# Weight rows in runs of four, x turned by every fourth column, and keys loaded as pairs of groups: one edit to a fused attention and expert kernel

## The chip, the cores and the metric

The kernel runs on one core of a Trainium2 chip. The metric is the device time of one execution in microseconds (us); lower is better. The kernel before takes 197.68 us in the median of three runs (197.22 to 197.88).

## The reference, cut to what matters

Attention over pooled keys and values, then a router that sends each row to one of eight experts, then that expert's two matrix products:

```python
# q, k, v: [8, 8, 576, 64] (batch, head, position, dim)
k_p = k.reshape(B, H, 72, 8, D).mean(axis=3)      # 72 groups of 8 positions
v_p = v.reshape(B, H, 72, 8, D).mean(axis=3)
attn = softmax(q @ k_p^T / sqrt(D))               # [576, 72] for each head
x = (attn @ v_p).transpose(0, 2, 1, 3).reshape(4608, 512)
...
logits = normalized(x) @ normalized(expert_emb).T / tau
e = argmax(logits); gate = softmax(logits)[e]
out[row] = gate * (relu(x[row] @ w1[e]) @ w2[e])  # w1 [8, 512, 1024], w2 [8, 1024, 512]
```

All inputs and the output are float32. The kernel works in float16 on the chip; the loads issued by POOL change the type on the way.

## The kernel before, in words

The work is done batch by batch (b = 0 to 7, 576 rows each). For a batch: V and K come as tiles of 72 partitions (one partition for each group of 8 positions), Q as 128 partitions. DVE adds up the 8 positions of a group (steps VA, VB for V, KA, KB for K; `halve` at L496, `k_fold` at L503). TensorE turns the pooled keys (step KT, `kt`, L606) and DVE copies them out of PSUM into the tile kpT (step KE, L622). Q is turned by DVE (QT, L595). Scores (SC, L636), exponentials on ACT (EX, L644), the product with V (PV, L682) and the normalization (XM, L410 and L411) give x, a tile of 128 rows by 512 columns in float16.

Five such chunks of x make a batch. `transpose_rows` (XT, L419) turns a chunk in four pieces of 128 columns: the piece is TensorE's stationary operand and an identity is streamed past it; `transpose_last` (L425) does the same for the last 64 rows. The copies XE put the turned pieces in xt, [128, 4, 576]. The router (RT, L434) multiplies pieces of xt with the turned expert table enT. An early guess of the batch's expert comes from the mean of the pooled values (GM, GL: `guess` at L565, also with enT), so that the weights can be asked for in good time.

The expert's layers: `h_mm` (H, L766) accumulates four products with a slice of w1 as the stationary operand and xt streamed; `h_relu` (HE) makes hT; `y_mm` and `yl_mm` (Y, YL; L778, L785) multiply hT with w2; YE scales the rows, and SP stores them (ST, SL). Weights sit in four slots for w1 and four for w2, keys, values and queries in two each.

The order of instructions on each engine is written out by hand in a table (TABLES: names of steps for PE, DVE, ACT, POOL and SP). A planner walks the table with estimated costs to choose buffers and, in the first 62 us, the number of filler products (`keep_warm`, L903, products of a tile of ones whose result nobody reads) ahead of a PE step that would wait. These numbers are fixed when the program is built. All loads are issued by POOL, in the order of its table; POOL's loads take eight completion semaphores in turn (DMASW0 to DMASW7), and a load waits until the load eight places before it has landed.

Of the kernel before, what the change touches and what calls it, by code (L numbers as in the profile page):

```python
# [260 lines left out]
def kernel(  # L261
# [27 lines left out]
    NW = 4  # L289
    ND = 2  # L290
# [13 lines left out]
    w2_r = [ring(f"w2{i}", 1, [128, 4, 2, DM], FP16) for i in range(NW)]  # L304
# [37 lines left out]
    enT = const.tile([128, 4, E], FP16)  # L342
# [73 lines left out]
    def transpose_rows(x, pt):  # L416
        xf = x.rearrange("p a r d -> p (a r d)")
        for w in range(4):
            nc.tensor.transpose(out=pt.bitcast(FP16)[:, ts(w, 128)], in_=xf[:, ts(w, 128)],  # L419
                                identity=ident_h)  # L420

    def transpose_last(x, pt):
        xf = x.rearrange("p a r d -> p (a r d)")
        for w in range(4):
            nc.tensor.matmul(out=pt[:, ts(w, 64)], lhsT=xf[:, ts(w, 128)],  # L425
                             rhs=ident_h[:, 64:128], start=True, stop=True)
# [28 lines left out]
    def attention(b, base, xt):  # L455
# [8 lines left out]
        for c, src, raw in (("V", v, vr), ("K", k, kr)):  # L464
            if b == 0:
                add(n(c, 0), 'POOL', 0.9, 0.0,
                    lambda src=src, raw=raw: load_rows(src, b, raw.tile, 0, 64),
                    takes=[raw], mode=(16, 2.78 if c == "V" else 2.7, 1.2), late=0.9)
                add(n(c, 1), 'POOL', 0.6, 0.0,
                    lambda src=src, raw=raw: load_rows(src, b, raw.tile, 64),  # L470
                    uses=[raw], mode=(8, 1.25 if c == "V" else 0.6, 1.2),
                    late=0.9 if c == "V" else 2.4)
            else:
                add(n(c), 'POOL', 0.8, 0.0,
                    lambda c=c, src=src, raw=raw: note(n(c), load_rows(src, b, raw.tile)),
                    takes=[raw], mode=wire(ROWS_DMA), late=1.1)
# [15 lines left out]
        def by_group(t):  # L492
            return t.rearrange("g (a h) (c e) -> g a h c e", a=NQ, c=2)
# [5 lines left out]
        def k_fold():  # L499
            t = kr.tile  # L500
            halve(t, 2)
            for a in range(NQ):
                nc.vector.tensor_tensor(  # L503
                    out=kp_rows()[:, a], in0=by_group(t[:, :, 0])[:, a],
                    in1=by_group(t[:, :, 1])[:, a], op=ALU.add)
# [96 lines left out]

        def kt(heads=range(NQ)):
            for a in heads:
                for c in range(2):
                    nc.tensor.transpose(  # L606
                        out=pk.tile.bitcast(FP16)[:, ts(2 * a + c, G)],
                        in_=kp.tile[:, a, c].rearrange("g h e -> g (h e)"),
                        identity=ident_h[0:G, 0:G])
# [10 lines left out]
        else:  # L620
            add(n("KT"), 'PE', 0.14, pr(0.0), kt, [n("KB"), "PRE"], takes=[pk], uses=[kp], late=0.22)
            add(n("KE"), 'DVE', 0.2, pr(-0.1), lambda: nc.vector.tensor_copy(  # L622
                out=kpT.tile[:, :, :, 0:G],
                in_=pk.tile.bitcast(FP16)[:, 0:2 * NQ * G].rearrange(
                    "p (a c g) -> p a c g", a=NQ, c=2)), [n("KT")], takes=[kpT], uses=[pk],
# [137 lines left out]
    def h_mm(xt, w1, w, c0, c1, p):  # L763
        w1v = w1.rearrange("p k (w c r) -> p k w r c", r=2, c=128)
        for kk in range(4):
            nc.tensor.matmul(out=p[:, 0:c1 - c0], lhsT=w1v[:, kk, w // 2, w % 2, :],  # L766
# [9 lines left out]
    def y_mm(hT, w2, c, p):  # L776
        for w in range(8):
            landing[f"Y{c}"] = nc.tensor.matmul(  # L778
                out=p, lhsT=hT[w][:, ts(c, 128)], rhs=w2[:, w // 2, w % 2, :],
                start=(w == 0), stop=(w == 7))  # L780

    def yl_mm(hT, w2, p, at=1):
        for w in range(8):
            for r in range(2):
                nc.tensor.matmul(out=p[ts(r, 64), ts(r * at, DH)],  # L785
                                 lhsT=hT[w][:, 512:S], rhs=w2[:, w // 2, w % 2, ts(r, DH)],
# [14 lines left out]
    def half_chunk(n, b, c, r, w2, hT, hs, g, o_b):  # L801
# [104 lines left out]
    def prelude():  # L906
# [30 lines left out]
        nc.vector.tensor_copy(out=enT, in_=p.bitcast(FP16)[:, 0:4 * E].rearrange(  # L937
            "p (w e) -> p w e", e=E))
# [237 lines left out]
```

## Time and the profile before

| | |
|---|---|
| median of three runs | 197.68 us (197.22 to 197.88) |
| the profiled execution's own time, and its span | 197.28 us, 195.7 us |
| mean granted TensorE clock | 0.997 |
| PE busy | 188.8 us (96%) |
| DVE, ACT, POOL busy | 148.1 us (76%), 126.8 us (65%), 42.4 us (22%) |
| loads issued by POOL (queue q0) | 21904 packets, 28.85 MB, 85.3% of 16 engines' time |

The span runs from the first to the last instruction; 1.6 us of the execution's time lie outside it. A matmul's recorded duration holds its whole way through the array, and matmuls follow each other sooner than that: how fast PE really works is read from the distance between the starts of rows in a timeline.

### The profile page before, as it was taken

What the parts mean: (1) busy time and instruction counts of PE and PEld (TensorE: products, weight loads), DVE (VectorE), ACT (ScalarE), POOL (GpSimd) and SP (SyncE); (2) the same over time, 40 slices, a digit from 0 to 9 for tenths busy, and PEclk for the clock granted to TensorE, in tenths of its full rate; (3) what the DMA queues carried; (4) which work ended last, traced back from release to release, by engine and by line L of the source; (5) the groups of instructions that cost most, each with busy time, mean ns of one, the idle gap of its engine ahead of it and who ended that gap; (6) DMA issues with size and microseconds to landing.
All of it is one profiled execution on the core that took longest, in us unless ns stands there. A gap on an engine that the chain in (4) does not pass through costs nothing.

```text
span 195.7 us, 5369 instructions
## 1 busy us (share of the span) xinstructions
PE 188.8 (96%) x2099; PEld 125.8 (64%) x2100; DVE 148.1 (76%) x428; ACT 126.8 (65%) x295; POOL 42.4 (22%) x59
## 2 busy tenths in 40 slices
PE   7999999999999999999999999999999999999990
PEld 4784787556865566656685567467765668567740
DVE  1266899499989799898989899599789437846750
ACT  4007637789787887769884868588866776156330
POOL 7445000530650023440410142011200302002000
PEclk9999999999999999999999999999999999999998
DMA  3999999999999999999999999999969699227762
GB/s 40 186 195 192 207 210 207 176 210 208 210 207 211 208 210 187 199 207 208 211 212 272 253 201 158 221 238 232 173 135 316 170 221 212 77 57 274 286 215 94
DMA packets 27982, 38.69 MB, mean 198 GB/s; under 512 B 4264, under 2 KB 14760, under 8 KB 27952
## 3 DMA queue, kind: packets, MB, share of 16 engines
q0 software_dynamic: 21904, 28.85, 85.3%
q1 hardware_dynamic: 5824, 9.26, 13.8%
q8 instruction: 17, 0.28, 0.5%
q10 hardware_dynamic: 224, 0.20, 0.4%
q14 instruction: 13, 0.11, 0.1%
HBM read 61.88 MB, written 9.44 MB: 364 GB/s over the span
## 4 chain that ended last, share of the span: by engine, by line
PE 87%; DVE 8%; issue 1%; ACT 1%; DVEq 0%
PE pb L766 26%; PE pb L778 22%; PE pa L766 7%; PE pb L903 7%; PE pa L636 6%; PE pa L682 5%; PE pb L785 3%; PE pb L419 3%; DVE qT L595 2%; PE pb L434 1%; PE pa L419 1%; DVE x L411 1%; DVE vr L496 1%; PE pa L778 1%; DVE kr L496 1%
## 5 line engine op out<-in xcount | busy, mean ns | idle before, releaser
L766 PEld LDWEIGHTS <-w 128*128 128x128 f16 x512 | 47.5, 98 | 14.6 <-issue 3.3
L778 PE MATMUL pb<-w,hT 128*128 128x512 f16 x240 | 56.6, 379 | 0.0
L766 PE MATMUL pb<-xt,w 128*128 128x288 f16 (+2 forms) x392 | 56.6, 286 | 0.0
L644 ACT ACTIVATE at<-pa 72x576 f16<-72x576 f32 (+2 forms) x64 | 38.6, 642 | 11.4 <-PE pa L636 11.2
L778 PEld LDWEIGHTS <-hT 128*128 128x128 f16 x248 | 22.6, 97 | 24.4 <-issue 1.7
L705 ACT ACTIVATE sq<-x 128x512 f16<-128x512 f16 x40 | 25.2, 629 | 10.2 <-DVE x L411 7.9
L791 ACT ACTIVATE y<-pb,gm_all 128x512 f32<-128x512 f32 (+2 forms) x34 | 21.2, 628 | 12.0 <-PE pb L778 4.8
L411 DVE TENSOR_TENSOR x<-pa,r_all 128x512 f16<-128x512 f32 x38 | 26.3, 691 | 2.2
L772 ACT ACTIVATE hT<-pb 128x288 f16<-128x288 f32 (+2 forms) x58 | 22.5, 411 | 6.0 <-PE pb L766 5.3
L595 DVE STREAM_TRANSPOSE qT<-qq 128x576 f16<-128x576 f16 x32 | 23.4, 754 | 0.0
L774 DVE TENSOR_SCALAR hT<-pb 128x288 f16<-128x288 f32 (+2 forms) x40 | 17.3, 450 | 7.3 <-PE pb L766 6.7
L445 POOL TENSOR_TENSOR ssq_all<-ssq_all,half_c 128x5 f32<-128x5 f32 x8 | 9.8, 1231 | 53.3 <-ACT sq L705 53.3
L766 PE MATMUL pa<-xt,w 128*128 128x288 f16 (+2 forms) x120 | 18.7, 285 | 0.0
L903 PE MATMUL pb<-ones_m 128*128 128x256 f16 x111 | 17.0, 305 | 1.5 <-DVE half_c L910 1.5
L682 PEld LDWEIGHTS <-at 72*128 72x128 f16 x320 | 13.6, 98 | 3.4 <-issue 1.6
L636 PE MATMUL pa<-qT,kpT 32*72 32x288 f16 (+2 forms) x256 | 15.5, 294 | 0.2
L496 DVE TENSOR_TENSOR vr<-vr 72x2048 f16<-72x2048 f16 (+1 forms) x16 | 15.0, 940 | 0.5 <-DMA vr<-in_v_dram 0.4
L682 PE MATMUL pa<-vpx,at 72*128 72x65 f16 x304 | 14.8, 194 | 0.0
L903 PEld LDWEIGHTS <-ones_m 128*128 128x128 f16 x114 | 11.3, 108 | 4.8 <-issue 1.4
L384 POOL DMA_DIRECT2D w<-in_moe_w_dram x8 | 5.5, 687 | 39.6 <-DVE xt L700 15.3
L496 DVE TENSOR_TENSOR kr<-kr 72x2048 f16<-72x2048 f16 (+1 forms) x14 | 13.2, 944 | 0.0
L772 ACT ACTIVATE hT<-pa 128x288 f16<-128x288 f32 (+2 forms) x23 | 9.0, 410 | 6.2 <-PE pa L766 6.1
(125 smaller groups left out, 202.3 us busy)
## 6 DMA issues: line engine op xcount, KB each, us to landing
w<-in_moe_w_dram POOLq DMA_DIRECT2D x16, 1024.0 KB, 13.3
out_dram<-y SPq DMA_DIRECT2D x31, 256.0 KB, 3.4
vr<-in_v_dram POOLq DMA_DIRECT2D x7, 576.0 KB, 13.7
kr<-in_k_dram POOLq DMA_DIRECT2D x7, 576.0 KB, 21.6
qq<-in_q_dram POOLq DMA_DIRECT2D x7, 576.0 KB, 12.4
out_dram<-y SPq DMA_DIRECT2D x15, 64.0 KB, 2.2
qq<-in_q_dram POOLq DMA_DIRECT2D x2, 288.0 KB, 7.6
vr<-in_v_dram POOLq DMA_DIRECT2D x1, 512.0 KB
```

The lines of the kernel that those rows point to most:

```text
L411: nc.vector.tensor_tensor(out=x[:, ts(i, np_)], in0=pxv[:, :, 1:129].rearrange("p a (r d) -> p a r d", d=D), in1=rv.unsqueeze(3).to_broadc ...
L496: nc.vector.tensor_tensor(out=t[:, :, 0:m], in0=t[:, :, 0:m], in1=t[:, :, m:2 * m], op=ALU.add)
L595: nc.vector.transpose(out=qT.tile[:, a].rearrange("p t c e -> p (t c e)")[:, cols], in_=qq.tile[:, a, cols]),
L636: nc.tensor.matmul(out=tiles[m // 2].tile[0:gs, m % 2 * 512:m % 2 * 512 + (p1 - p0) * T], lhsT=kpT.tile[ts(m, R), a, c, 0:gs], rhs=qT.tile ...
L644: nc.scalar.activation(out=t.tile[:, :, p0 * T:p1 * T].rearrange("g r (p t) -> g r p t", t=T), in_=p.tile[0:G].rearrange("g (r c) -> g r c ...
L682: nc.tensor.matmul(out=px[h // 2 // np_].tile[:, o:o + 65], lhsT=at[h // 2].tile[:, h % 2, c0:c0 + 128], rhs=vp.tile[:, h // 2, 1 + h % 2 ...
L705: nc.scalar.activation(out=sq, in_=x.tile.rearrange("p a r d -> p (a r d)"), func=AF.Square, accum_out=ssq_all[:, b, c:c + 1])
L766: nc.tensor.matmul(out=p[:, 0:c1 - c0], lhsT=w1v[:, kk, w // 2, w % 2, :], rhs=xt[:, kk, c0:c1], start=(kk == 0), stop=(kk == 3))
L772: nc.scalar.activation(out=dst, in_=src, func=AF.Relu)
L778: landing[f"Y{c}"] = nc.tensor.matmul(out=p, lhsT=hT[w][:, ts(c, 128)], rhs=w2[:, w // 2, w % 2, :], start=(w == 0), stop=(w == 7))
L791: nc.scalar.activation(out=dst, in_=src, func=AF.Copy, scale=g)
L903: nc.tensor.matmul(out=p[:, 256:512], lhsT=ones_m[:, 0:128], rhs=ones_m[:, 0:256], start=True, stop=True)
```

## The change

Three layouts change together.

- w1 is loaded as "(p w) f -> p w f" in place of "(w p) f -> p w f": partition p holds rows 4p to 4p+3, one run of 16 KB in memory, and not four rows that lie 128 rows apart. So piece w of x must hold columns w, w+4, w+8 and so on: the transposes take every fourth column of x, and so does the router's table (enT). The guess still works on columns in their old order and gets a table of its own (enG).
- w2 is loaded with four rows in a run (8 KB) in place of two (4 KB), and `h_mm` takes every fourth column of a slice of w1 in place of every second one, so that hT's rows come in w2's order.
- Keys of batches 1 to 7 come in two transfers of 36 partitions each (heads 0 to 3, heads 4 to 7). A partition holds a pair of neighbouring groups for four heads, so that a run is 4 KB and not 2 KB. After the turn the groups of a pair lie in two halves of the PSUM tile, and two copies (`unpair`) put them back side by side.

The engines' tables and the planner's rules stay; one cost is raised (KE from 0.2 to 0.35).

```diff
+    NR = 4
-    w2_r = [ring(f"w2{i}", 1, [128, 4, 2, DM], FP16) for i in range(NW)]
+    w2_r = [ring(f"w2{i}", 1, [128, 8 // NR, NR, DM], FP16) for i in range(NW)]
...
-    enT = const.tile([128, 4, E], FP16)
+    enT, enG = (const.tile([128, 4, E], FP16, name=f"en{i}") for i in range(2))
...
+    def load_pairs(b, raw):
+        for s in range(2):
+            ld = nc.gpsimd.dma_start(
+                out=raw.rearrange("p (h a) t d -> p h (a t d)", a=2)[ts(s, G // 2)],
+                in_=k[b][ts(s, QG)].rearrange("h (j r) d -> j h (r d)", j=G // 2))
+        return ld
...
-            in_=moe_w1[ds(e_val, 1)].squeeze(0).rearrange("(w p) f -> p w f", p=128),
+            in_=moe_w1[ds(e_val, 1)].squeeze(0).rearrange("(p w) f -> p w f", w=4),
...
-                "(w p r) d -> p w r d", p=128, r=2),
+                "(w p r) d -> p w r d", p=128, r=NR),
...
     def transpose_rows(x, pt):
-        xf = x.rearrange("p a r d -> p (a r d)")
+        xf = x.rearrange("p a r d -> p (a r d)").rearrange("p (c w) -> p w c", w=4)
         for w in range(4):
-            nc.tensor.transpose(out=pt.bitcast(FP16)[:, ts(w, 128)], in_=xf[:, ts(w, 128)],
+            nc.tensor.transpose(out=pt.bitcast(FP16)[:, ts(w, 128)], in_=xf[:, w],
                                 identity=ident_h)
...
-                                 rhs=enT[:, w, :], start=(w == 0), stop=(w == 3))
+                                 rhs=enG[:, w, :], start=(w == 0), stop=(w == 3))
...
+        def unpair():
+            src = pk.tile.bitcast(FP16)[:, 0:4 * G].rearrange(
+                "p (a c s j) -> p a s c j", a=2, c=2, s=NQ)
+            dst = kpT.tile[:, :, :, 0:G].rearrange("p s c (j a) -> p a s c j", a=2)
+            for a in range(2):
+                nc.vector.tensor_copy(out=dst[:, a], in_=src[:, a])
...
-            add(n("KE"), 'DVE', 0.2, pr(-0.1), lambda: nc.vector.tensor_copy(
-                out=kpT.tile[:, :, :, 0:G],
...
+            add(n("KE"), 'DVE', 0.35, pr(-0.1), unpair, [n("KT")], takes=[kpT], uses=[pk],
                 late=0.1)
...
-        w1v = w1.rearrange("p k (w c r) -> p k w r c", r=2, c=128)
+        w1v = w1.rearrange("p k (w c r) -> p k w r c", r=NR, c=128)
...
         for w in range(4):
-            nc.tensor.transpose(out=p.bitcast(FP16)[:, ts(w, E)], in_=emb_h[:, ts(w, 128)],
-                                identity=ident_h[:E, :E])
+            for r, cols in enumerate((emb_h[:, ts(w, 128)],
+                                      emb_h.rearrange("e (c w) -> e w c", w=4)[:, w])):
+                nc.tensor.transpose(out=p.bitcast(FP16)[:, ts(4 * r + w, E)], in_=cols,
+                                    identity=ident_h[:E, :E])
```

What stands on the engines is nearly the same before and after. On PE the prelude has eight small transposes of the expert table in place of four; everything else, the filler products too, stands in the same order and number. ACT and SP are unchanged. POOL has seven transfers more. Three places follow.

POOL, the loads of batches 1 to 3, before (w_67, w_68: w1; w_71: w2; in brackets the semaphores it waits for):

```order
L384 DMA w_67<-in_moe_w_dram 128x4x1024
L361 DMA kr_76<-in_k_dram 72x8x512 [waits DMASW0_49]
L367 DMA qq_80<-in_q_dram 128x2x1152 [waits DMASW1_49]
L390 DMA w_71<-in_moe_w_dram 128x4x1024 [waits DMASW2_49]
L361 DMA vr_77<-in_v_dram 72x8x512 [waits DMASW3_49,DVE_49,PE_49]
L361 DMA kr_75<-in_k_dram 72x8x512 [waits DMASW4_49,PE_49]
L384 DMA w_68<-in_moe_w_dram 128x4x1024 [waits DMASW5_49]
```

and now:

```order
L392 DMA w_67<-in_moe_w_dram 128x4096
L368 DMA kr_76<-in_k_dram 36x4x1024 [waits DMASW0_49]
L368 DMA kr_76<-in_k_dram 36x4x1024 [waits DMASW1_49]
L375 DMA qq_80<-in_q_dram 128x2x1152 [waits DMASW2_49]
L398 DMA w_71<-in_moe_w_dram 128x2x2048 [waits DMASW3_49]
L362 DMA vr_77<-in_v_dram 72x8x512 [waits DMASW4_49,DVE_49,PE_49]
L368 DMA kr_75<-in_k_dram 36x4x1024 [waits DMASW5_49,PE_49]
L368 DMA kr_75<-in_k_dram 36x4x1024 [waits DMASW6_49]
L392 DMA w_68<-in_moe_w_dram 128x4096 [waits DMASW7_49]
```

The order of the loads is kept; each load of keys is two, and all that come behind take later semaphores.

DVE, where the keys of batch 2 are copied out of PSUM (step KE2, tile kpT_85), before:

```order
L774 TENSOR_SCALAR hT_99<-pb_63 128x288
L622 COPY kpT_85<-pa_61 128x4x72
L595 STREAM_TRANSPOSE qT_81<-qq_79 128x576 x3
L774 TENSOR_SCALAR hT_99<-pb_63 128x288
L774 TENSOR_SCALAR hT_107<-pb_64 128x288
```

and now:

```order
L787 TENSOR_SCALAR hT_99<-pb_63 128x288
L617 COPY kpT_85<-pa_61 128x4x36 x2
L604 STREAM_TRANSPOSE qT_81<-qq_79 128x576 x3
L787 TENSOR_SCALAR hT_99<-pb_63 128x288
L787 TENSOR_SCALAR hT_107<-pb_64 128x288
```

One copy of 288 elements becomes two of 144, at the same place ahead of the last three turns of Q.

DVE, the same step for batch 3 (KE3, tile kpT_86), before:

```order
L411 TENSOR_TENSOR x_96<-pa_62,r_all 128x512
L595 STREAM_TRANSPOSE qT_82<-qq_80 128x576
L622 COPY kpT_86<-pb_63 128x4x72
L496 TENSOR_TENSOR vr_78<-vr_78 72x8x256
L793 TENSOR_SCALAR y_117<-pb_65,gm_all 128x512
```

and now:

```order
L419 TENSOR_TENSOR x_96<-pa_62,r_all 128x512
L604 STREAM_TRANSPOSE qT_82<-qq_80 128x576
L617 COPY kpT_86<-pb_63 128x4x36 x2
L505 TENSOR_TENSOR vr_78<-vr_78 72x8x256
L806 TENSOR_SCALAR y_117<-pb_65,gm_all 128x512
```

Here the copies come behind the turn of Q that the first scores of the batch need.

## Rows read from the trace of the kernel before

**Rows 1.** The page, part 4: share of the last chain by engine.

```profile
PE 87%; DVE 8%; issue 1%; ACT 1%; DVEq 0%
```

**Rows 2.** Windows: length; PE, PEld, DVE, ACT, POOL busy; clock; DMA share; GB/s.

```profile
70.00:120.00 50.00, 50.00 (x568) 33.61 (x567) 46.11 (x124) 38.09 (x89) 14.95 (x19) 1.00 1.16 212
120.00:170.00 50.00, 50.00 (x585) 32.79 (x584) 37.74 (x111) 35.51 (x83) 5.36 (x6) 1.00 0.94 203
```

**Rows 3.** Waits: who waited for whom; us in total, times, longest.

```profile
PEld L419 <- DVE x L411: 0.8, 2, 0.5
...
PEld L636 <- DVE qT L595: 0.6, 2, 0.3
...
PEld L636 <- DVE kpT L622: 0.3, 1, 0.3
...
PE pa L419 <- DVE mv L584: 0.4, 1, 0.4
...
DVE vr L496 <- DMA vr<-in_v_dram: 0.4, 1, 0.4
```

**Rows 4.** PE startup in the timeline: start, us, instruction.

```profile
6.70 0.26 PE L935 MATMUL pb<-ident_h,x 8*128 8x8 f16 x4
6.90 2.15 PE L903 MATMUL pb<-ones_m 128*128 128x256 f16 x18
```

**Rows 5.** DVE groups by form: busy, mean ns of one | idle before.

```profile
L622 DVE COPY kpT<-pb 128x288 f16<-128x288 f16 x5 | 1.4, 283 | 0.0
...
L774 DVE TENSOR_SCALAR hT<-pb 128x320 f16<-128x320 f32 x2 | 1.0, 477 | 0.0
L774 DVE TENSOR_SCALAR hT<-pb 128x256 f16<-128x256 f32 x2 | 0.8, 418 | 0.3 <-PE pb L766 0.3
...
L615 DVE COPY kpT<-pb 128x144 f16<-128x144 f16 x2 | 0.3, 199 | 0.0
```

**Rows 6.** Timeline around the first scores of batch 2.

```profile
53.05 2.08 DVE L595 STREAM_TRANSPOSE qT<-qq 128x576 f16<-128x576 f16 x3
...
53.95 0.15 PEld L636 LDWEIGHTS <-kpT 32*72 32x72 f16 x8 [0.24 <-DVE qT L595]
```

**Rows 7.** Timeline around the first scores of batch 3.

```profile
69.01 0.27 DVE L622 COPY kpT<-pb 128x288 f16<-128x288 f16 x1
...
69.33 0.15 PEld L636 LDWEIGHTS <-kpT 32*72 32x72 f16 x8 [0.28 <-DVE kpT L622]
```

**Rows 8.** PE weight loads by form: busy, mean ns of one | idle before.

```profile
L766 PEld LDWEIGHTS <-w 128*128 128x128 f16 x512 | 47.5, 98 | 14.6 <-issue 3.3
...
L419 PEld LDWEIGHTS <-x 128*128 128x128 f16 x128 | 8.2, 97 | 3.0 <-DVE x L411 0.8 <-issue 0.6
```

**Rows 9.** PE timeline: transposes of batch 0, and the router of batch 4.

```profile
25.22 0.39 PE L419 MATMUL pa<-ident_h,x 128*128 128x128 f16 x4
25.44 0.28 PE L425 MATMUL pb<-ident_h,x 128*128 128x64 f16 x4
25.56 0.60 PE L766 MATMUL pa<-xt,w 128*128 128x256 f16 x4
...
109.58 0.64 PE L434 MATMUL pb<-enT,xt 128*128 128x8 f16 x20
110.08 0.24 PE L565 MATMUL pb<-enT,mv 128*128 128x8 f16 x4
```

**Rows 10.** DMA queue of 15.0:15.6 and of 18.98:19.4: packets, MB, share of 16 engines.

```profile
q0 software_dynamic: 89, 0.09, 90.9%
...
q0 software_dynamic: 45, 0.09, 115.8%
```

**Rows 11.** The first w2: POOL's issue, its time to landing, and its first reader.

```profile
15.02 0.80 POOL L390 DMA_DIRECT2D w<-in_moe_w_dram  x1
...
w<-in_moe_w_dram POOLq DMA_DIRECT2D x1, 1024.0 KB, 20.2
...
36.02 1.89 PE L778 MATMUL pb<-w,hT 128*128 128x512 f16 x8
```

More of the change, by code (lines that the diff above doesn't have):

```diff
@@ L416, in transpose_rows @@
     def transpose_rows(x, pt):
-        xf = x.rearrange("p a r d -> p (a r d)")
+        xf = x.rearrange("p a r d -> p (a r d)").rearrange("p (c w) -> p w c", w=4)
         for w in range(4):
-            nc.tensor.transpose(out=pt.bitcast(FP16)[:, ts(w, 128)], in_=xf[:, ts(w, 128)],
+            nc.tensor.transpose(out=pt.bitcast(FP16)[:, ts(w, 128)], in_=xf[:, w],
                                 identity=ident_h)
     def transpose_last(x, pt):
-        xf = x.rearrange("p a r d -> p (a r d)")
+        xf = x.rearrange("p a r d -> p (a r d)").rearrange("p (c w) -> p w c", w=4)
         for w in range(4):
-            nc.tensor.matmul(out=pt[:, ts(w, 64)], lhsT=xf[:, ts(w, 128)],
+            nc.tensor.matmul(out=pt[:, ts(w, 64)], lhsT=xf[:, w],
                              rhs=ident_h[:, 64:128], start=True, stop=True)
@@ L474, in attention @@
                 add(n(c), 'POOL', 0.8, 0.0,
-                    lambda c=c, src=src, raw=raw: note(n(c), load_rows(src, b, raw.tile)),
+                    lambda c=c, src=src, raw=raw: note(n(c), load_pairs(b, raw.tile) if c == "K"
+                                                       else load_rows(src, b, raw.tile)),
                     takes=[raw], mode=wire(ROWS_DMA), late=1.1)
@@ L490, in vp_rows, with by_pair @@
             return vp.tile[:, :, 2:130]
-        def by_group(t):
-            return t.rearrange("g (a h) (c e) -> g a h c e", a=NQ, c=2)
+        def by_pair(t):
+            return t.rearrange("p (h a) (c e) -> p a h c e", a=2, c=2)
         def halve(t, m):
@@ L503, in k_fold @@
                 nc.vector.tensor_tensor(
-                    out=kp_rows()[:, a], in0=by_group(t[:, :, 0])[:, a],
-                    in1=by_group(t[:, :, 1])[:, a], op=ALU.add)
+                    out=kp_rows()[:, a], in0=by_pair(t[:, :, 0])[:, a],
+                    in1=by_pair(t[:, :, 1])[:, a], op=ALU.add)
         def v_fold():
@@ L621, in attention @@
             add(n("KT"), 'PE', 0.14, pr(0.0), kt, [n("KB"), "PRE"], takes=[pk], uses=[kp], late=0.22)
-            add(n("KE"), 'DVE', 0.2, pr(-0.1), lambda: nc.vector.tensor_copy(
-                out=kpT.tile[:, :, :, 0:G],
-                in_=pk.tile.bitcast(FP16)[:, 0:2 * NQ * G].rearrange(
-                    "p (a c g) -> p a c g", a=NQ, c=2)), [n("KT")], takes=[kpT], uses=[pk],
+            add(n("KE"), 'DVE', 0.35, pr(-0.1), unpair, [n("KT")], takes=[kpT], uses=[pk],
                 late=0.1)
@@ L763, in h_mm @@
     def h_mm(xt, w1, w, c0, c1, p):
-        w1v = w1.rearrange("p k (w c r) -> p k w r c", r=2, c=128)
+        w1v = w1.rearrange("p k (w c r) -> p k w r c", r=NR, c=128)
         for kk in range(4):
-            nc.tensor.matmul(out=p[:, 0:c1 - c0], lhsT=w1v[:, kk, w // 2, w % 2, :],
+            nc.tensor.matmul(out=p[:, 0:c1 - c0], lhsT=w1v[:, kk, w // NR, w % NR, :],
                              rhs=xt[:, kk, c0:c1], start=(kk == 0), stop=(kk == 3))
@@ L778, in y_mm @@
             landing[f"Y{c}"] = nc.tensor.matmul(
-                out=p, lhsT=hT[w][:, ts(c, 128)], rhs=w2[:, w // 2, w % 2, :],
+                out=p, lhsT=hT[w][:, ts(c, 128)], rhs=w2[:, w // NR, w % NR, :],
                 start=(w == 0), stop=(w == 7))
@@ L785, in yl_mm @@
                 nc.tensor.matmul(out=p[ts(r, 64), ts(r * at, DH)],
-                                 lhsT=hT[w][:, 512:S], rhs=w2[:, w // 2, w % 2, ts(r, DH)],
+                                 lhsT=hT[w][:, 512:S], rhs=w2[:, w // NR, w % NR, ts(r, DH)],
                                  start=(w == 0), stop=(w == 7))
@@ L807, in mm @@
                 nc.tensor.matmul(out=p.tile[:, 0:DH], lhsT=hT[w].tile[:, ts(c, 128)],
-                                 rhs=w2.tile[:, w // 2, w % 2, cols],
+                                 rhs=w2.tile[:, w // NR, w % NR, cols],
                                  start=(w == 0), stop=(w == 7))
@@ L934, in prelude @@
         for w in range(4):
-            nc.tensor.transpose(out=p.bitcast(FP16)[:, ts(w, E)], in_=emb_h[:, ts(w, 128)],
-                                identity=ident_h[:E, :E])
-        nc.vector.tensor_copy(out=enT, in_=p.bitcast(FP16)[:, 0:4 * E].rearrange(
-            "p (w e) -> p w e", e=E))
+            for r, cols in enumerate((emb_h[:, ts(w, 128)],
+                                      emb_h.rearrange("e (c w) -> e w c", w=4)[:, w])):
+                nc.tensor.transpose(out=p.bitcast(FP16)[:, ts(4 * r + w, E)], in_=cols,
+                                    identity=ident_h[:E, :E])
+        for r, t in enumerate((enG, enT)):
+            nc.vector.tensor_copy(out=t, in_=p.bitcast(FP16)[:, 4 * r * E:4 * (r + 1) * E].rearrange(
+                "p (w e) -> p w e", e=E))
     ext = const.tile([1, B, E], FP32)
```

## The prediction

> **What bounds the kernel now.** I read the chain that ended last first: 87% of it is PE's own work and 8% DVE's; no transfer has a share [rows 1]. The windows say the same from the other side: from 70 to 170 us PE is busy all the time at full clock, while the DMA engines, too, are nearly full up to 120 us (a share above 1 means that packets overlap) [rows 2]. Two resources are full, so the question is which one the other waits for. The table of waits answers it: in the whole span one compute instruction waits for a load, and that for 0.4 us, on DVE. What PE waits for is DVE, in short pieces: 0.8 us for x, 0.6 for turned queries, 0.3 for turned keys, 0.4 for a mean [rows 3]. So the loads are full but early, and a faster load by itself buys nothing. From about 23 us on, the end is set by how many instructions PE has and how closely they follow each other, plus some 2 us of waits for DVE. Ahead of that, fillers of a fixed number stand where PE would wait; a fixed number doesn't shrink when the data come earlier.
>
> **What the change costs, part by part.**
>
> *Prelude.* Four small transposes more. The four of before lie between the starts at 6.70 and 6.90 [rows 4], 50 ns each, so four more push all fillers behind them, and with them the first real products, by 0.2 us. The products behind the fillers need V's load as well; if they wait for it already, a part is hidden. I take 0.15, with 0.05 and 0.2 as the ends. The second table's copy on DVE lies beside the fillers and costs nothing; without them it would cost its own short duration once.
>
> *Keys out of PSUM (KE).* In seven batches one copy of 128x288 (283 ns) becomes two of 128x144. Rows of that size exist: 199 ns each, so 398 for a pair, 0.12 more, if nothing of the two overlaps [rows 5]. What no row shows is the new write: every second element. Copies in float16 grow by (283 - 199) / 144 = 0.58 ns for an element, the operations on float32 of 256 and 320 columns by (477 - 418) / 64 = 0.92 [rows 5]. At the slower pace two copies of 144 take 98 ns more, and the step 0.21 more than before. From below nothing is left if the pair overlaps well. I take 0.12, the nearest rows as they stand, and keep 0 and 0.21.
>
> On that point a rule speaks against the change. The Trainium skill, VectorE: DVE Perf Modes, section "What auto-detection actually checks", says that the doubled pace of 16-bit data wants every tensor at a step of one. By it the pair loses the doubled pace and the sum below would have 0.21 in place of 0.12 for each exposed step. The rows bear out the doubled pace (0.58 against 0.92); none shows a step of two.
>
> Which of the seven are exposed? Only where PE waits for DVE right behind. In batch 3 the scores wait 0.28 us for this very copy [rows 7]. In batch 2 they wait 0.24 for the turn of Q, and that stands directly behind the copy on DVE, with the three turns merged in one row without a gap [rows 6]. The third wait, for a turn of Q in batch 0, has no changed copy ahead of it. In the other five batches PE doesn't wait for either [rows 3], since the copy is done while PE multiplies. So 2 x 0.12 = 0.24 on the path, with 0 and 0.42 as ends. Without that cover the other five would add 0.6.
>
> *Transposes of x, and w1 as a stationary operand.* The same number of instructions, the same columns. New is the step of the stationary operand: four in place of one for x, four in place of two for w1. A weight load with a step of two (w1) takes 98 ns, one with a step of one (x) 97 [rows 8]: no difference. What could be hidden is how soon the next may follow. The router's products, eight columns each, follow each other at 0.50 / 20 = 25 ns, so a weight load needs no more than that; transposes stand at 0.22 / 4 = 55 ns, those of the last chunk at 0.12 / 4 = 30 [rows 9]. A load with a step of four may thus take twice as long before full transposes notice. I take nothing, and treat the rest as a rival.
>
> *The loads.* Two windows in which nearly all packets have one size: 89 packets of 1 KB with 90.9% of 16 engines over 0.6 us, that is 98 ns each; 45 of 2 KB with 115.8% over 0.42 us, 173 ns each [rows 10]. So 23 ns for a packet and 75 for each KB. If each longer run becomes one packet, w1 saves 384 packets a load, w2 256, keys 288; seven loads of each move data (24 loads of 0.59 MB and 14 of 1.05 make the queue's 28.85 MB). 928 x 7 x 23 ns / 16 engines = 9.3 us of the DMA engines' time at most; if runs are cut into packets as before, nothing. Since PE waits for no load, I put it at nothing for the time, and keep the one DVE wait, 0.4 us, as what it can give directly [rows 3].
>
> *POOL.* Seven more issues, each at most as long as the issue of a w2, 0.80 us [rows 11]. POOL is busy 15.0 of 50 us and 5.4 of 50 [rows 2], so this is hidden, except where loads are issued one behind the other. The tightest place is the first w2: issued at 15.02, landed 20.2 later at 35.2, and first read at 36.02 [rows 11], 0.8 us of slack. One more issue ahead of it uses up 0.80 at most. The semaphores go round faster too, but a load then waits for one eight places before it, which at these distances has mostly landed.
>
> *Sum.* 0.15 + 0.24 = 0.39 us. On the profiled execution's own 197.28 us (span 195.7 and 1.6 outside) that gives 197.7. That execution lies at the low end of the runs, whose median is 197.68; on the median it gives 198.1. I take the middle, **197.9 us**. The likeliest case by itself has the ends 0.05 and 0.62: 197.3 to 198.3.
>
> **The rivals.**
>
> *Loads that land earlier are worth something after all (faster).* For it: the DMA engines are the only other full resource, and 9.3 us of theirs may come free. DVE's wait of 0.4 us for V would go, and steps of DVE that follow a load could run earlier, so that PE's waits for DVE (0.8 + 0.6 + 0.3 + 0.4 = 2.1 us) shrink [rows 3]. Against: none of those waits stands on a load in its row. If half of them and the 0.4 go and the prelude's 0.15 stays, the time falls by 1.05 + 0.4 - 0.15 = 1.3: 196.4; with a quarter of them 196.9.
>
> *DVE has no slack anywhere (slower).* DVE is busy 46.1 of 50 us in the middle [rows 2]. If the copy is exposed in all seven batches and at the slow pace, 7 x 0.21 + 0.15 = 1.6: 199.3. It decides when PE's waits for kpT appear in more than four batches. Against it: only one such wait now [rows 3].
>
> *A weight load with a step of four is slower (slower).* It decides at 30 ns for a load: then the 32 transposes of the last chunks are stretched, at 50 ns by 20 each, 0.6 us, which with the sum is 198.5 or a little more. From 55 ns on the 128 others are stretched too; at 100 ns (four times the 25) 128 x 45 + 32 x 70 = 8.0 us, 205.9. Against it: a step of two costs nothing [rows 8].
>
> *Loads that land later (slower).* If the two transfers of keys hold up what is behind them by more than the 0.8 us of slack, PE waits for the first w2 [rows 11]; at 1 us over the slack, 198.7 + 0.4 = 199.1. Against it: the queue behind them is full, so an issue later by 0.8 need not land later. The Trainium skill speaks for this one in DMA: Bandwidth & Descriptors, "Rules for kernel authors": it advises against two transfers to two halves of the partitions, since they share the same engines. No row here has such a pair.
>
> **How the numbers follow.** A measurement of this kernel can tell about 0.3%, 0.6 us, from no change: 197.1 to 198.3. Chances: the sum 0.56, earlier loads 0.16, DVE without slack 0.10, slower weight loads 0.12 (most of it at the small price), later loads 0.06. Of the sum's 0.56, 0.02 lie above 198.3; of the earlier loads, a quarter lies above 197.1. So faster 0.13, no change 0.59, slower 0.28. The range 196.9 to 199.0 leaves out half of the earlier loads, the dear end of the weight loads and the upper half of DVE's rival, 0.18 in all.
>
> **What would show it right or wrong.** In the profile of the changed kernel: the distance between starts of transposes still 55 and 30 ns; PE's fillers at the start 0.1 to 0.2 us later; pairs of copies of 0.3 to 0.5 us for KE, and the waits of the scores in batches 2 and 3 longer by about 0.1 each; packets of q0 fewer by up to 6500, and PE's waits still without a load. I am wrong if PE's transposes spread, if PE waits for w or kpT in several batches, or if PE's waits for x and qT vanish together with DVE's wait for V. Longer packets could also hold up SP's stores; at the end no load is in flight, so I expect nothing of that.

## The result and the profile after

The changed kernel takes 198.92 us (median of 7 runs, 198.51 to 199.89 without one) against 197.68 for the kernel before on the same chip: a ratio of 1.0068, 95% interval 1.0042 to 1.0094. One of the seven runs took 1035.98 us; it is left out of the ratio, and why it did isn't known. The profiled execution took 198.62 us, its span is 197.0 (195.7 before).

The page of the changed kernel, part 4 and the row of the load queue, and the windows of [rows 2] (length; PE, PEld, DVE, ACT, POOL busy; clock; DMA share; GB/s):

```profile
PE 78%; DVE 14%; issue 3%; POOL 1%; ACT 1%; POOLq 0%; DVEq 0%; ACTq 0%
```

```profile
q0 software_dynamic: 14848, 28.85, 81.9%
```

```profile
70.00:120.00 50.00, 50.00 (x570) 36.22 (x563) 46.45 (x126) 37.74 (x88) 15.94 (x22) 1.00 1.12 210
120.00:170.00 50.00, 49.94 (x586) 35.39 (x585) 37.47 (x110) 36.21 (x86) 4.91 (x6) 1.00 0.90 201
```

DVE's share of the last chain has grown from 8 to 14% [rows 1]. The queue moves the same 28.85 MB in 14,848 packets, 7,056 fewer than before, and its share of the engines falls from 85.3 to 81.9%; but the rate in the two windows is 210 and 201 GB/s, no higher than the 212 and 203 of before [rows 2]. Nothing arrives faster.

The waits of PE and of PEld, its weight loads (us in total, times, longest), which answer to [rows 3]:

```profile
PE pb L916 <- DVE half_c L923: 1.5, 1, 1.5
PE pa L427 <- DVE x L419: 0.4, 1, 0.4
PE pa L649 <- DVE kpT L617: 0.3, 1, 0.3
PE pb L975 <- DVE ohb L971: 0.2, 1, 0.2
PE pb L779 <- DVE kpT L617: 0.2, 1, 0.2
```

```profile
PEld L427 <- DVE x L419: 1.1, 3, 0.5
...
PEld L649 <- DVE kpT L617: 0.5, 1, 0.5
PEld L649 <- DVE qT L604: 0.3, 1, 0.3
```

No row of PE or DVE waits for a load any more: DVE's 0.4 us for V is gone. The wait for the turned keys has grown from 0.3 to 0.5, a wait of h_mm (L779) for that copy is new, and PEld's waits for x are three and not two, 1.1 us and not 0.8. DVE's timeline around the copy of batch 3, which answers to [rows 7], and PE's beside it (start, length, instruction):

```profile
68.57 0.77 DVE L604 STREAM_TRANSPOSE qT<-qq 128x576 f16<-128x576 f16 x1
69.26 0.50 DVE L617 COPY kpT<-pb 128x144 f16<-128x144 f16 x2
69.67 1.20 DVE L505 TENSOR_TENSOR vr<-vr 72x2048 f16<-72x2048 f16 x1
```

```profile
69.13 0.39 PE L427 MATMUL pb<-ident_h,x 128*128 128x128 f16 x4
69.81 0.44 PE L649 MATMUL pa<-qT,kpT 32*72 32x288 f16 x8 [0.30 <-DVE kpT L617]
```

The pair takes 0.50 us where the one copy took 0.27, and PE stands still for it. All fourteen copies by themselves (duration min/median/max in ns, first and last start in us):

```profile
L617 DVE COPY kpT<-pb x10: 277/305/319, 32.0 to 147.7; 128x144 f16<-128x144 f16 x10
L617 DVE COPY kpT<-pa x4: 285/308/319, 52.9 to 91.3; 128x144 f16<-128x144 f16 x4
```

Half the columns take longer than all of them did before (305 against 283 ns, [rows 5]). The weight loads by form (count, busy us, mean ns), which answer to [rows 8]:

```profile
L779 PEld LDWEIGHTS <-w 128*128 128x128 f16 x512 | 55.2, 114 | 7.9 <-issue 3.5
...
L427 PEld LDWEIGHTS <-x 128*128 128x128 f16 x128 | 8.9, 114 | 3.1 <-DVE x L419 1.1 <-issue 0.6
```

Both step-of-four loads went from 98 and 97 to 114 ns.

Where the time is lost shows when the start of each PE instruction is compared with the same instruction of the kernel before. The table gives by how much PE is late, in us from the span's start, as the median over the instructions of a stretch (times of the kernel before), here and for the traces of the experiments below. Each trace is of one execution: those of only_pairs and plain_halves, 198.83 and 198.44 us, lie below the medians that are given with them.

| kernel | 6.7-7 | 24-32 | 33-53 | 55-69 | 70-90 | 90.5-91.4 | 94-107 | 115-146 | 148-170 | 185-191 |
|---|---|---|---|---|---|---|---|---|---|---|
| the change | -0.33 | -0.19 | 0.04 | 0.25 | 0.51 | 0.58 | 0.80 | 0.84 | 1.20 | 1.25 |
| no_pairs | 0.11 | 0.26 | 0.26 | 0.33 | 0.38 | 0.41 | 0.47 | 0.44 | 0.58 | 0.62 |
| only_pairs | -0.03 | -0.04 | 0.20 | 0.35 | 0.57 | 1.40 | 1.39 | 1.38 | 1.60 | 1.61 |
| v_order | 0.12 | 0.25 | 0.26 | 0.33 | 0.38 | 0.56 | 0.62 | 0.59 | 0.73 | 0.78 |
| ke_twice | 0.00 | -0.02 | 0.33 | 0.60 | 1.06 | 1.07 | 1.40 | 1.51 | 1.86 | 1.87 |
| plain_halves | 0.12 | 0.27 | 0.34 | 0.39 | 0.49 | 0.81 | 0.87 | 0.83 | 1.03 | 1.07 |
| only_nr | -0.39 | -0.37 | -0.37 | -0.32 | -0.28 | -0.28 | -0.23 | -0.31 | -0.22 | -0.20 |
| only_x | -0.34 | -0.01 | -0.01 | 0.01 | 0.01 | 0.04 | 0.03 | -0.05 | 0.00 | 0.02 |
| pairs_v_order | -0.49 | -0.36 | -0.36 | -0.36 | -0.36 | 0.11 | 0.10 | -0.01 | -0.01 | -0.01 |
| pairs_plain | 0.00 | 0.11 | 0.12 | 0.13 | 0.13 | 1.82 | 1.81 | 1.70 | 1.69 | 1.70 |
| halves | -0.41 | -0.42 | -0.41 | 0.24 | 0.25 | 2.56 | 3.91 | 3.79 | 3.80 | 3.80 |
| halves_both | -0.47 | -0.47 | -0.47 | -0.31 | -0.31 | 0.83 | 0.83 | 0.71 | 0.71 | 0.72 |
| ke_split | 0.00 | -0.01 | 0.23 | 0.31 | 0.25 | 0.25 | 0.24 | 0.39 | 0.55 | 0.56 |

In the change five steps stand out: 0.23 at 32.5 (batch 1), 0.21 at 54 (batch 2), 0.26 at 69 (batch 3), 0.22 at 91.5 (batch 4) and 0.36 at 147 (batch 7). Each lies where the turned keys leave PSUM. The first column is mostly no part of the change: the pace of the fillers ahead of it differs from one execution to the next (last section), by more than the 0.13 us of the four added transposes.

### The profile page after: what moved, and what is told of

Its sections match the earlier page's. It is cut to its first block, busy times and chain, and to the rows that moved or that the text cites. A ratio compares the mean times of both kernels' runs of the same rounds, so it can differ in the third digit from the quotient of the medians.

```text
span 197.0 us, 5397 instructions
## 1 busy us (share of the span) xinstructions
PE 189.4 (96%) x2103; PEld 134.2 (68%) x2104; DVE 149.6 (76%) x436; ACT 126.9 (64%) x295; POOL 43.8 (22%) x66
## 3 DMA queue, kind: packets, MB, share of 16 engines
q0 software_dynamic: 14848, 28.85, 81.9%
## 4 chain that ended last, share of the span: by engine, by line
PE 78%; DVE 14%; issue 3%; POOL 1%; ACT 1%; POOLq 0%; DVEq 0%; ACTq 0%
PE pb L779 23%; PE pb L791 22%; PE pa L649 6%; PE pa L779 5%; PE pb L916 4%; PE pa L695 4%; PE pb L798 3%; DVE qT L604 3%; PE pb L427 2%; DVE vr L505 2%; DVE kr L505 2%; DVE x L419 1%; PE pb L442 1%; DVE kpT L617 1%; PE pa L791 1%
## 5 line engine op out<-in xcount | busy, mean ns | idle before, releaser
L779 PEld LDWEIGHTS <-w 128*128 128x128 f16 x512 | 55.2, 114 | 7.9 <-issue 3.5
L779 PE MATMUL pb<-xt,w 128*128 128x288 f16 (+2 forms) x392 | 56.8, 287 | 0.2 <-DVE kpT L617 0.2
L657 ACT ACTIVATE at<-pa 72x576 f16<-72x576 f32 (+2 forms) x64 | 38.5, 641 | 12.3 <-PE pa L649 11.9
L419 DVE TENSOR_TENSOR x<-pa,r_all 128x512 f16<-128x512 f32 x38 | 26.3, 692 | 2.2
L779 PE MATMUL pa<-xt,w 128*128 128x288 f16 (+2 forms) x120 | 18.7, 285 | 0.0
L916 PE MATMUL pb<-ones_m 128*128 128x256 f16 x111 | 16.4, 297 | 1.5 <-DVE half_c L923 1.5
L649 PE MATMUL pa<-qT,kpT 32*72 32x288 f16 (+2 forms) x256 | 15.6, 294 | 0.4 <-DVE kpT L617 0.3
L392 POOL DMA_DIRECT2D w<-in_moe_w_dram x8 | 4.1, 509 | 39.1 <-DVE xt L713 15.6
```

Source lines behind the costliest of these rows:

```text
L419: nc.vector.tensor_tensor(out=x[:, ts(i, np_)], in0=pxv[:, :, 1:129].rearrange("p a (r d) -> p a r d", d=D), in1=rv.unsqueeze(3).to_broadc ...
L649: nc.tensor.matmul(out=tiles[m // 2].tile[0:gs, m % 2 * 512:m % 2 * 512 + (p1 - p0) * T], lhsT=kpT.tile[ts(m, R), a, c, 0:gs], rhs=qT.tile ...
L657: nc.scalar.activation(out=t.tile[:, :, p0 * T:p1 * T].rearrange("g r (p t) -> g r p t", t=T), in_=p.tile[0:G].rearrange("g (r c) -> g r c ...
L779: nc.tensor.matmul(out=p[:, 0:c1 - c0], lhsT=w1v[:, kk, w // NR, w % NR, :], rhs=xt[:, kk, c0:c1], start=(kk == 0), stop=(kk == 3))
L916: nc.tensor.matmul(out=p[:, 256:512], lhsT=ones_m[:, 0:128], rhs=ones_m[:, 0:256], start=True, stop=True)
```

## The experiments

Theory 1: the pairs of copies on DVE are what costs. Theory 2: the step of four in PE's stationary operands. Theory 3: the transfers of keys in halves disturb the loads. The code orders of PE, DVE and ACT are the same as in the kernel that each run starts from, except for the copies and turns that it edits; POOL's differ by the transfers alone. Ratios are to the kernel before as it ran beside each experiment, with medians of 197.25 to 197.44 us.

**no_pairs**: the change without its keys.

```diff
-   note(n(c), load_pairs(b, raw.tile) if c == "K" else load_rows(src, b, raw.tile))
+   note(n(c), load_rows(src, b, raw.tile))
-   add(n("KE"), 'DVE', 0.35, pr(-0.1), unpair, ...)
+   add(n("KE"), 'DVE', 0.2, pr(-0.1), lambda: nc.vector.tensor_copy(  # one copy, as before
```

> The changed kernel with the keys loaded and copied as in the kernel before (one transfer, one copy of 128x288), the weights and the turn of x still as in the change. Theory 1 (the pair of copies on DVE is what costs: each pair ends about 0.22 us later than the one copy, and PE waits for that in five batches): the 1.0 us goes, time 197.7 to 198.0, PE without a wait over 0.1 us more than before at the keys of batches 1, 2, 3, 4 and 7. Theory 2 (the step of four in PE's stationary operands costs): the time stays at 198.6 to 198.9. Theory 3 (the transfers in halves disturb what runs beside them): as theory 1, so this run doesn't tell 1 from 3.

198.01 us, ratio 1.0034 (1.0016 to 1.0052). In the table the steps at batches 1 to 4 shrink to 0.07 at most and the one at 147 to 0.14. The change loses 1.58 from its first column to its last, this kernel 0.51, so the keys cost 1.07 us: theory 1, or 3. Of that, 0.23, 0.14, 0.21, 0.16 and 0.22, in all 0.96, stand at the five places. The 0.51 are the weights and the turn of x, of which 0.14 come at 21 us, where the first chunk of x is turned. Weight load and DVE in the kernel before, then in no_pairs:

```profile
20.84 0.41 PEld L419 LDWEIGHTS <-x 128*128 128x128 f16 x4
```

```profile
20.66 0.42 DVE L411 TENSOR_TENSOR x<-pb,r_all 128x256 f16<-128x256 f32 x1
```

```profile
21.25 0.26 PEld L420 LDWEIGHTS <-x 128*128 128x128 f16 x4 [0.31 <-DVE x L412]
```

```profile
20.77 0.42 DVE L412 TENSOR_TENSOR x<-pb,r_all 128x256 f16<-128x256 f32 x1
```

DVE makes this chunk in two halves of 256 columns, and these rows are the second half. Two of the old pieces lie in the first half, so PE began them while DVE was at the second; every fourth column takes from both, so now all four pieces wait for its end.

**only_pairs**: the kernel before with the change's `load_pairs`, `by_pair` and `unpair` and nothing else.

```diff
+   note(n(c), load_pairs(b, raw.tile) if c == "K" else load_rows(src, b, raw.tile))
+   add(n("KE"), 'DVE', 0.35, pr(-0.1), unpair, ...)
```

> The kernel before with the change's keys alone: two transfers of 36 partitions and the pair of copies. Theory 1: 197.7 + 1.0 = 198.7, with the step at each of the five places 0.15 to 0.25 us. Theory 2: 197.7, no change. Theory 3: 198.7, but the lost time stands beside transfers and not at the copies.

199.68 us, ratio 1.0116 (1.0088 to 1.0144): more than any theory gave. The steps at batches 1, 2, 3 and 7 are there (0.23, 0.15, 0.22, 0.21), as theory 1 has it. But 0.83 come at 90.5, and that isn't a copy. PE's waits and its timeline there:

```profile
PE pb L778 <- DMA w<-in_moe_w_dram: 0.7, 1, 0.7
```

```profile
91.84 1.03 PE L778 MATMUL pb<-xt,w 128*128 128x288 f16 x7 [0.66 <-DMA w<-in_moe_w_dram]
```

The w1 that is first read there was issued at 79.44 and landed 12.4 us later; in the kernel before it was issued at 78.87 and landed 10.9 us later, at 89.8, for a first read at 90.4. So some 0.7 us of slack were there, and the halves use them up. Theory 3 is alive beside theory 1. In the full change the same w1, now in longer runs, was issued at 79.37 and landed at 90.96, and its first reader starts at 91.01:

```profile
91.01 0.88 PEld L779 LDWEIGHTS <-w 128*128 128x128 f16 x8
```

No wait shows there, but of the slack 0.05 us are left.

**v_order**: the change with one copy and V in the keys' order.

```diff
-   for a in range(2):
-       nc.vector.tensor_copy(out=dst[:, a], in_=src[:, a])     # dst "(j a)": every second element
+   nc.vector.tensor_copy(out=dst, in_=src)                     # dst "(a j)": runs of 36
+   def load_split(b, raw):                                     # V: groups 2j+a in partitions a*36+j
+       for a in range(2):
+           ld = nc.gpsimd.dma_start(out=raw...[ts(a, G // 2)],
+               in_=v[b].rearrange("h (j a t) d -> a j h (t d)", a=2, t=POOL)[a])
```

> The changed kernel with the pairs of keys left in the order in which they come, so that one copy of 128x288 with whole runs of 36 takes the pair's place, and V loaded in that same order of groups, in two transfers of 36 partitions as well. The result is the same, since the order of the keys doesn't matter to the sum. Theory 1: the copy takes 0.28 us again and about 1.0 us goes: 197.7 to 198.0. Theory 2: stays at 198.6 to 198.9. Theory 3: stays or grows to 199.5, since there are now twice as many transfers in halves.

197.90 us, ratio 1.0020 (0.9995 to 1.0046): theory 1's figure. The copy is the old length again, though it reads and writes in pieces of 36:

```profile
L623 DVE COPY kpT<-pb x5: 267/291/298, 32.5 to 147.3; 128x288 f16<-128x288 f16 x5
```

and the steps at batches 1 to 4 are those of no_pairs, except 0.18 at 90.5, where a w1, issued at 79.2, lands 11.7 us later, just when it is read. The run changes two things at once, though: V, too, comes in halves, and that matters by itself (halves and halves_both, below). So the gain in time isn't shown to be the copy's alone.

**ke_twice**: the kernel before with its one copy made twice.

```diff
+   def ke():
+       for _ in range(2):
+           nc.vector.tensor_copy(out=kpT.tile[:, :, :, 0:G], in_=pk...)   # the same copy
```

> The kernel before with the one copy of the turned keys made twice in each of the seven batches, and nothing else changed. A second copy ends about 0.2 us later (between starts of neighbouring copies), as the pair does. Theory 1: the delay shows in the same five batches, 0.15 to 0.25 us in each, 198.6 to 198.9 in all. Theories 2 and 3: as before, 197.7.

199.25 us, ratio 1.0096 (1.0065 to 1.0126). A longer copy by itself, with every load as before, loses in the same five places: 0.34, 0.27, 0.46, 0.34, 0.34, and 0.1 more beside them. That is more than I expected, and so is the delay: the two copies take 0.61 to 0.64 us, 0.34 more than the one, and not 0.2. Its waits name what is late:

```profile
PE pa L640 <- DVE kpT L605: 0.5, 1, 0.5
...
PE pb L770 <- DVE kpT L605: 0.3, 1, 0.3
...
PE pb L419 <- DVE kpT L605: 0.2, 1, 0.2
```

Only L640, the scores, wants the keys. L770 (h_mm, batch 1) and L419 (turns of x, batch 7) write a PSUM buffer and are released by the copy that reads one: they wait for the bank that the copy holds. In batch 4 it is the queue behind the copy: two copies of xt follow it on DVE, and PE's scores wait for the second of them, which frees the bank that they write, in the kernel before (first row) as in the change:

```profile
91.53 0.16 PEld L636 LDWEIGHTS <-kpT 32*72 32x72 f16 x8 [0.24 <-DVE xt L700]
```

```profile
91.08 0.50 DVE L617 COPY kpT<-pa 128x144 f16<-128x144 f16 x2
91.49 0.41 DVE L713 CAST xt<-pb 128x256 f16<-128x256 f32 x1
91.82 0.41 DVE L713 COPY xt<-pa 128x512 f16<-128x512 f16 x1
```

```profile
92.11 0.31 PEld L649 LDWEIGHTS <-kpT 32*72 32x72 f16 x8 [0.22 <-DVE xt L713]
```

**plain_halves**: the change with both copies writing whole runs.

```diff
-   dst = kpT.tile[:, :, :, 0:G].rearrange("p s c (j a) -> p a s c j", a=2)
+   dst = kpT.tile[:, :, :, 0:G].rearrange("p s c (a j) -> p a s c j", a=2)
```

> The changed kernel with the two copies of the keys writing whole runs of 36 in place of every second element, so that the keys stand in another order than V (its output is not the reference's). If the step of the writing is what makes a copy long, each takes 0.20 us and the pair 0.40 in place of 0.52; with 0.12 less in five batches the time falls by 0.6 to 198.2 or so. If it is the pieces in which both read PSUM, the pair stays at 0.5 and the time at 198.7.

```profile
L617 DVE COPY kpT<-pb x10: 190/214/222, 32.5 to 147.6; 128x144 f16<-128x144 f16 x10
```

214 in place of 305 ns: the step of the writing makes a copy long, not the pieces and not the number. A pair now takes 0.33 us from first start to last end, and the steps of batches 1 to 4 fall to 0.07, 0.06, 0.10 and 0.06. The time didn't follow: 198.85 us, ratio 1.0088 (1.0063 to 1.0114), where 198.2 was expected. In its trace 0.32 at 90.5 (w1 again) and a later start take the gain's place:

```profile
91.24 0.76 PEld L779 LDWEIGHTS <-w 128*128 128x128 f16 x7 [0.26 <-DMA w<-in_moe_w_dram]
```

Its loads are the change's, and its w1 is issued at 79.35 and lands at 91.2; that the change itself shows no wait is a matter of 0.05 us. Whether w1 is all of the missing gain isn't shown: the execution traced is faster than the median.

**only_nr** and **only_x**: the two parts of the weights, each alone on the kernel before.

```diff
+   NR = 4                                        # only_nr: w2 in runs of four, w1's columns by four
-   in_=moe_w1[...].rearrange("(w p) f -> p w f", p=128)     # only_x, with enG and x by fours
+   in_=moe_w1[...].rearrange("(p w) f -> p w f", w=4)
```

> The kernel before with w2 in runs of four rows and the columns of w1 read with a step of four; keys, rows of w1 and x as before. Theory 2 (a weight load with a step of four slows PE): the loads of w1 take 114 ns in place of 98, and the distance of h_mm's products grows, by 512 x 16 ns = 8 us at most. Against it: the products behind them stand 123 ns apart already, which hides 114, so 197.4 to 197.7, no change.

> The kernel before with the rows of w1 in runs of four, x turned by every fourth column and the second table of the experts; w2, the columns of w1 and the keys as before. Theory 2: the prelude's 0.18, 32 turns of the last chunks at 35 in place of 29 ns (0.2) and 0.1 to 0.2 behind the other turns: 0.5 us, the same as the weights and the turn of x together, so 197.9 to 198.2. If w1's columns carry that loss, 197.6 to 197.8.

197.38 us (1.0001, 0.9973 to 1.0029) and 197.57 us (1.0013, 0.9986 to 1.0039): neither can be told from no change. In the first, w1's loads take 114 ns and PE loses 0.19 us from the first column to the last; in the second, x's take 114 to 117 and PE loses 0.36, of it 0.33 ahead of the second column: 0.17 at 11.9 us, where PE, early by its fast fillers, waits for a load of keys, and 0.15 at 21 us, as in no_pairs. Theory 2 falls as the main cause.

**pairs_v_order**, **pairs_plain** and **halves**: the transfers of the keys without the long copies. The first is v_order's keys and V on the kernel before; the second loads the keys as pairs, with one plain copy; the third cuts K's old transfer into two.

```diff
+   def load_halves(b, raw):                      # halves
+       for s in range(2):
+           ld = load_rows(k, b, raw, s * G // 2, (s + 1) * G // 2)
```

> The kernel before with keys loaded as pairs, one copy of 128x288 for them, and V loaded in the same order of groups; weights and x as before. The pair of copies is gone, so what is left is the transfers in halves. Theory 1 by itself (all of the loss is DVE's copies): 197.4 to 197.7, as the kernel before. Theory 3, in the form that the keys alone showed (a w1 that lands late, PE waiting 0.8 us for it near 90 us): 198.2 to 198.6, with PE's wait for w in the trace and no other step over 0.1 us.

> The kernel before with the keys loaded as pairs and one plain copy of 128x288 for them, V as before (so the keys stand in another order than V, and the output is not the reference's): the two transfers without what the copies cost. If the late w1 comes with the transfers, PE waits for w near 90 us by 0.3 to 0.8 as in the run with the pairs and their copies: 197.8 to 198.3; if it needs the copies' delay too, 197.4 to 197.6.

> The kernel before with K's seven transfers cut into two of 36 partitions each, in the order and the pieces of 1 KB of before; one copy for the turned keys, everything else as before. If it is the halves (one more issue, 36 partitions in a transfer) that make the w1 near 90 us land late, PE waits for w there, 0.3 to 0.8 us, and the time is 197.8 to 198.3. If it is the pairs' longer runs, no wait for w: 197.4 to 197.6. Theory 1 (DVE's copies are all): 197.4 to 197.6.

197.54 us (1.0016, 0.9992 to 1.0039), 199.75 (1.0119, 1.0080 to 1.0159) and 201.71 (1.0240, 1.0203 to 1.0276). Theory 3's figure for the first was too high, though its trace loses 0.47 at 90.5 to a wait for w; pairs_plain, whose PE arrives there earlier than with the long copies, waits 1.5 us and loses 1.69. Cutting K alone costs far more than the whole change. Of halves: PE's waits, its timeline at 90 us, and windows behind it (columns as in [rows 2]):

```profile
PE pb L772 <- DMA w<-in_moe_w_dram: 2.1, 1, 2.1
...
PE pb L784 <- DMA w<-in_moe_w_dram: 0.5, 1, 0.5
```

```profile
90.48 0.39 PE L424 MATMUL pa<-ident_h,x 128*128 128x128 f16 x4
93.01 1.16 PE L772 MATMUL pb<-xt,w 128*128 128x288 f16 x8 [2.14 <-DMA w<-in_moe_w_dram]
```

```profile
93.00:94.00 1.00, 0.99 (x8) 0.70 (x8) 0.00 (x0) 0.29 (x1) 0.05 (x1) 1.00 1.17 210
94.00:95.00 1.00, 1.00 (x30) 0.69 (x29) 0.00 (x0) 0.92 (x3) 0.00 (x0) 0.78 1.13 213
95.00:96.00 1.00, 1.00 (x12) 0.64 (x10) 0.68 (x4) 1.00 (x3) 0.00 (x0) 0.50 1.11 210
96.00:97.00 1.00, 1.00 (x5) 0.41 (x3) 1.00 (x2) 0.36 (x2) 0.55 (x1) 0.50 1.14 216
97.00:98.00 1.00, 1.00 (x11) 0.43 (x11) 1.00 (x2) 0.61 (x2) 1.00 (x2) 0.51 1.10 209
98.00:99.00 1.00, 1.00 (x10) 0.80 (x9) 0.94 (x3) 0.99 (x3) 0.74 (x2) 1.00 1.10 207
```

PE waits 2.1 us for w1, and 1.5 us after it has begun again its granted clock falls to half, 1.2 GHz, for 3.4 us: 2.32 us are lost at 90.5 and 1.34 more in the stretch behind it. The 0.5 us at L784 are an earlier wait, for a w2 at 58 us, which costs 0.66. The Trainium skill, DMA: Bandwidth & Descriptors, "Rules for kernel authors", advises against two transfers to two halves of the partitions. These runs agree where K alone is in halves, by 2.4% with short runs and 1.2% with pairs; with K and V both in halves the loss is 0.2% (pairs_v_order, not clear of no change) and 0.5% (halves_both).

**halves_both**: K and V both in halves, to see whether it is the number of transfers.

```diff
-   note(n(c), load_halves(b, raw.tile) if c == "K" else load_rows(src, b, raw.tile))
+   note(n(c), load_halves(src, b, raw.tile))
```

> The kernel before with both K and V cut into two transfers of 36 partitions each, pieces of 1 KB and everything else as before; so 14 more transfers, where the run with K alone in halves had 7 more and lost 4 us. If more transfers and more issues are what make the w1 near 90 us late, the loss grows: 201.7 or more. If it is how uneven the transfers fill the 16 DMA engines (a theory: a transfer of 72 or of 36 partitions goes over 12 of them, the next begins where the last ended, as the kernel's own table of costs has it; with K alone in halves the engines' backlogs drift apart by 5 us, with both in halves by 2 or less, worked out so from the issues of the kernel before), the w1 lands as in the kernel before: 197.2 to 197.8, PE without a wait for w over 0.3 us.

198.12 us, ratio 1.0049 (1.0024 to 1.0074). Twice as many extra transfers lose a fifth as much, so their number isn't it. My theory of unevenly filled engines isn't confirmed either: PE still waits 1.0 us for w there. Why w1 lands late with K in halves stays open; the trace doesn't tell which engine moved a packet.

**ke_split**: the kernel before with half of its copy on ACT.

```diff
+   for a, copy in enumerate((nc.vector.tensor_copy, nc.scalar.copy)):
+       copy(out=kpT.tile[:, a, :, 0:G], in_=pk...)
```

> The kernel before with half of the copy of turned keys on ACT and half on DVE in each of the seven batches: DVE's part falls from 0.28 to 0.20 us. Theory 1 in reverse: where PE waited already (batches 2 and 3) up to 0.08 us is gained each, elsewhere nothing, since the other three only cost once their slack is used up: 197.2 to 197.4, if ACT takes its half at once. If ACT is late with it, behind its exponentials of 0.64 us, PE waits longer and the time rises to 198 and above.

197.97 us, ratio 1.0031 (1.0013 to 1.0050): slower by 0.3%. ACT's half takes 279 ns and begins after DVE's, so the pair ends later than the one copy, and PE loses 0.24 at batch 1 and 0.16 at batch 7, where the bank comes free with the later half. No version run here is faster than the kernel before.

## Why the prediction was wrong

I forecast 197.9 us and no measurable change; it is 198.92, just inside my range of 196.9 to 199.0, and slower by more than the measurement's uncertainty. The step that failed is the one on the keys, **"Which of the seven are exposed? Only where PE waits for DVE right behind"**, and with it a size.

- *Which are exposed.* I counted batches 2 and 3, because there PE's waits named the turned keys or the turn of Q behind them [rows 6, 7]. Five lose (2, 3, and 1, 4, 7). I asked only who reads what the copy writes. The copy also holds the bank that it reads, which h_mm takes next in batch 1 and the turns of x in batch 7, and it stands ahead of the copies of xt that release the scores in batch 4. "The copy is done while PE multiplies" was true of the keys and not of the bank and the queue. ke_twice shows the five places with nothing else changed, and in the change's own trace no row of PE waits for a load.
- *The size.* I took 0.12 and kept 0.21 as the dear end; a pair takes 0.49 to 0.53 us where one copy took 0.26 to 0.30, 0.23 more. What I took as the likelier was a row for copies without a step. That the dear end is so near is in part luck: I had each copy 49 ns longer and no overlap; measured, each is 106 ns longer (305 against 199), but the second starts 0.19 to 0.22 us after the first, so they overlap by 0.1. Without the step a pair would have cost 0.06 to 0.07 (plain_halves). By the Trainium skill, VectorE: DVE Perf Modes, section "What auto-detection actually checks", the step costs the doubled pace; 305 ns with it and 214 without agree. At the five places 0.96 us are lost; I had 0.24.
- *The rival that came true* is that of DVE without slack, which had 0.10 and 199.3. Its sign for deciding was waits for kpT in more than four batches; the trace has such rows in two (1 and 3), though five lose, because in batches 2 and 4 PE waits for what stands behind the copy in DVE's queue (qT, xt), and in batch 7 it stands idle for only 0.06 us.
- *The prelude*: 0.15 forecast. Where the fillers speed up no earlier than 6.6 us, the ones behind the small transposes begin at 7.02 to 7.03 with eight of them and at 6.87 to 6.90 with four, so 0.13 is measured.
- *Transposes of x*: I took nothing, since I asked only how long a load with a step takes. What I missed is what a piece needs: columns from both halves of a chunk that DVE makes half by half, 0.14 us in batch 0.
- *Weight loads with a step of four*: I had no difference; they take 16 to 17 ns longer, below the 30 at which I let it decide. The 32 turns of the last chunks stand 35 ns apart in place of 29, 0.2 us at most; full turns stand at 56 as before, h_mm's products at 123. From the second column to the last no_pairs loses 0.36, of which only_nr shows 0.17 and only_x 0.03; the rest stays open.
- *The loads*: no gain, as forecast, and the DVE wait of 0.4 went without a trace in the time. But "a faster load buys nothing" hid that a later one costs. I put the slack of the first w2 at 0.8 us and looked no further; the w1 at 90 us has 0.7, and K in halves uses more than that. The rival of later loads was right in its mechanism, though the change shows no wait for it: w1 lands 11.6 us after its issue there (10.9 before, 12.4 in only_pairs), so the longer runs may make up for a part, and the rest just fits into the slack. Packets fell by 7,056, more than the 6,500 that I allowed, and by the page's shares the queue's packets take some 5.6 us of engine time less (an estimate), where I had 9.3 at most. I also overlooked a second wait for a load, 0.4 us of ACT for the expert table at the start; both kernels have it.
- *POOL*: the issues stayed hidden, as forecast. One load was held for 3.0 us by the semaphores' round, until 91.24, and nothing waits for it.

## What to carry to other kernels

Before an instruction is called covered, ask three things of it: who reads its output, who takes the buffer that it reads from, and what stands behind it on its engine; a wait table answers only with the last of these that came late. Ask of a new order, too, which part of its input each piece needs, and when that is ready. Pay for a new data order where it costs no step in the writing: let the order stand and give the partner the same order (V here), rather than put it right element by element. When a part of a change is found harmless, look how much slack it has used up: K alone in halves cost 1 to 2% on the kernel before; in the change it leaves 0.05 us of w1's 0.7, and a run with the same loads waits 0.3.

## What was not expected of the hardware

- A DVE copy in float16 of 128x144 from PSUM that writes every second element took 305 ns; with whole runs of 36 it took 214, and 128x288 with whole runs 283 to 291.
- A weight load of 128x128 in float16 with a step of four took 114 to 117 ns in place of 97 to 98; a step of two had cost nothing.
- 7,056 packets fewer left the queue's rate where it was: 210 and 201 GB/s against 212 and 203.
- The fillers at the start, products of 256 columns that run from 1.5 us on, stand 0.21 us apart and from some point on 0.11, the pace of 1.2 and then of 2.4 GHz by these numbers. The trace's record of the granted clock begins at that point, with full clock: at 6.95 us in the kernel before, 5.46 in the change, 4.60 in pairs_v_order. The windows print 1.00 for the time ahead of it as well, for which there is no record. The point differs from execution to execution and moves a single profile by up to 0.5 us (the table's first column).
